# An emission order written out as a table, the mixing shifts on compute engines, and W3 loaded ahead, in a gated long-convolution and MLP-mixer kernel

## The chip, the cores and the metric

The kernel runs on one core of one Trainium2 chip. The metric is the device time in microseconds (us) of one execution. A core has five engines, each with an in-order instruction queue of its own: TensorE (PE in the profile, with its weight loads as PEld), VectorE (DVE), ScalarE (ACT), GpSimd (POOL) and SyncE (SP). In this kernel SP issues every transfer. Engines wait for one another through semaphores.

## The reference, cut to what matters

With S = 2048 positions, D = 640 channels and F = 1536 hidden channels, in bf16:

```python
x = A_q
g = sigmoid((x * gate_w).sum(-1, keepdims=True))
# A: a 4-tap shift convolution of k, times v, then a causal long convolution over S
k_shift = sum(k_pad[:, t:t + S, :] * shift_k[:, 3 - t] for t in range(4))
kv = k_shift * v
y = irfft(rfft(kv, 2S) * rfft(ssm_k, 2S))[:S] + kv * ssm_D
a = x * y
# B: a token mixer and an MLP, each with a residual
h = gelu(layernorm(x) @ w1)             # four groups of 160 channels
hs = concat(h shifted by 1, -1, 2, -2 positions, group by group) @ w2
x1 = x + hs
b = x1 + gelu(layernorm(x1) @ w3) @ w4
out = g * a + (1 - g) * b
```

## The kernel before, in words

Positions are laid out as 128 partitions by 16 slabs, so a slab is 128 rows of 640 channels. The work falls into two arms that share x and meet at the output. Every operation is a node with a short name, and the names are those of the table in the change.

**The mixer arm.** `q0` to `q7` load x into QX. `st0.s` takes the statistics of slab s, on DVE or on ACT; `rs0.s` forms the inverse deviation of two slabs on POOL; `xn0.s` normalizes on DVE into a ring of three XN buffers. `tr0.c.i` transposes two slabs on PE and `te0.c.i` copies the result out of PSUM, for four chunks c of four slabs each. `W1.c.n` is a 128x512 tile of x @ w1, five matmuls each, and `g1.c.n` is its gelu on ACT. The last 32 channels of each 160-channel group are gathered in MIX, and `mx c.gi` brings them into GST at their shifted position (lines 828 to 833: twenty small SBUF-to-SBUF transfers issued by SP). `W2.s` multiplies a slab by w2 (ten matmuls) and `add s` adds it to x on DVE. `gt.c`, `z c` and `gate0` to `gate2` make the gate.

**The MLP.** `st1`, `rs1` and `xn1` normalize again; `xt1.c.i` transposes a slab by a DMA transpose (line 757) into one of two XNT buffers; `W3.c.f` (line 967) are 48 tiles of five matmuls 128x512; `g2.c.f` their gelus; `W4.s.j` (line 980) 32 tiles of twelve matmuls 128x320; `w4e s.j` (line 986) adds them into QX on DVE. `xo s` scales x1 by 1 - g beforehand. `w3` and `w4` load the weights into the tile W34.

**The convolution.** A two-level Fourier transform as matmuls. Its tables are generated on the chip: `ang`, `and`, `abs` and `sin` fill F1, `m3*` fill M3; the scratch for the angles lies in W34. `trh` (line 914) transposes the filter, `trhe` copies it out, `h1.s.h` (line 936) is its first level, `he` copies it out and `hw c` writes it to DRAM. `km` (lines 1024 and 1029), `ka` (line 1033) and `kv` (line 1036) form kv on DVE, eight operations of 1280 columns for each pair of slabs; `x1`, `xe` and `xw` are the first level of kv. `rh` and `rx` (line 1080) read both spectra back in another layout; `h2` and `x2` (line 1053) are the second level; `sw` (line 1096) swaps partition neighbours by a transfer; `pq` (line 1113) multiplies the spectra on DVE; `pv` (line 1053) is the first inverse level; `ve` copies it out; `vw` writes it to DRAM and `rv` reads it back. `iv s` (line 1149) is the last inverse level of slab s, four matmuls; `y s` (line 1154) multiplies it by the gate and by x, which `rq` (line 1141) has loaded again; `ya s` (line 1159) adds it into QX; `st s` stores the slab.

**What sets the order.** `Plan.schedule` is a list scheduler that runs when the program is built. It gives each node a rank from due times (`PAR`) and from 928 corrections (`ADJ`), keeps for each engine the nodes that are ready, and at each step starts the ready node of lowest rank on a free engine; it also chooses ACT or DVE or POOL where a node has alternatives, and the buffer of each ring. All transfers share one model of a DMA path at a node's rate, with 350 ns to issue and 1900 ns of latency. The nodes are then emitted in the order of their modelled starts, so each engine's queue has that order. PSUM is a ring of eight banks; a tile `w=2` takes two neighbours.

Of the kernel before, what the change touches and what calls it, by code (L numbers as in the profile page):

```python
# [20 lines left out]
class Ring:  # L21
    def __init__(self, name, n):
        self.name, self.n = name, n
        self.free = list(range(n))


    def take(self, w):
        if w == 1:
            one = [i for i in self.free if self.n != 8 or i ^ 1 not in self.free] or self.free
            i = min(one)  # L30
            self.free.remove(i)
            return i
        i = min(i for i in self.free if i % 2 == 0 and i + 1 in self.free)
        self.free.remove(i)
        self.free.remove(i + 1)
        return i

    def can(self, w, keep):
        if len(self.free) < w + keep:
            return False  # L40
        return w == 1 or any(i % 2 == 0 and i + 1 in self.free for i in self.free)


class Buf:
    __slots__ = ("ring", "idx", "users", "gate", "w")

    def __init__(self, ring, gate=(), w=1):
        self.ring, self.idx, self.users, self.gate, self.w = ring, None, 0, tuple(gate), w


class Node:
    __slots__ = ("name", "alts", "fn", "deps", "succ", "bufs", "mode", "tgt", "after", "bytes", "rate",
                 "npend", "ready", "start", "end", "eng", "rank", "seq", "lat", "sts")


DMA_ISSUE = 350.0
DMA_LAT = 1900.0


def lat_of(n):  # L60
    return 230.0 if "PE" in n.alts else (60.0 if n.bytes else 170.0)


class Plan:
# [3 lines left out]
    def add(self, name, alts, fn, deps=(), bufs=(), mode=None, tgt=None, after=0.0, nbytes=0, rate=370.0):  # L68
# [8 lines left out]
        n.bufs, n.mode, n.tgt, n.after, n.bytes, n.rate = list(bufs), mode, tgt, after, nbytes, rate  # L77
        n.seq = len(self.nodes)
        self.nodes.append(n)
        return n  # L80

    def dma(self, name, fn, nbytes, deps=(), bufs=(), q="SP", rate=370.0, tgt=None, after=0.0):
        return self.add(name, {q: DMA_ISSUE}, fn, deps, bufs, None, tgt, after, nbytes, rate)

    def schedule(self, par):
        nodes = self.nodes
        rings, bufs = {}, {}
        for n in nodes:
            n.succ, n.eng, n.start, n.end = [], None, None, None
            for b in n.bufs:  # L90
                bufs[id(b)] = b
                rings[id(b.ring)] = b.ring
                b.users, b.idx = 0, None
        for r in rings.values():
            r.free = list(range(r.n))
        for n in nodes:
            for b in n.bufs:
                b.users += 1
            n.npend = len(n.deps)
            n.ready = n.after  # L100
            n.lat = lat_of(n)
            for d in n.deps:
                d.succ.append(n)
        topo, cntp = [n for n in nodes if not n.deps], {id(n): len(n.deps) for n in nodes}
        for n in topo:
            for s in n.succ:
                cntp[id(s)] -= 1
                if cntp[id(s)] == 0:
                    topo.append(s)
        assert len(topo) == len(nodes)  # L110
        for n in reversed(topo):
            dur = min(n.alts.values())
            if n.bytes:
                dur += DMA_LAT + n.bytes / n.rate
            n.rank = min((s.rank for s in n.succ), default=400000.0) - n.lat - dur
            if n.tgt is not None:
                g = par[n.tgt[0]]
                n.rank = min(n.rank, 1000.0 * (g[0] + sum(x * y for x, y in zip(g[1:], n.tgt[1:]))))
        for n in nodes:
            if "PE" in n.alts:  # L120
                for d in n.succ:
                    if "PE" not in d.alts and any(b.ring.name == "ps" and b in n.bufs for b in d.bufs):
                        d.rank = min(d.rank, n.rank + 1000.0 * par["evac"][0])
        for i, (a, _) in ADJ.items():
            nodes[i].rank += 1000.0 * a
        keep = int(par["keep"][0] + 0.5)
        vpen, mpen = 1000.0 * par["vpen"][0], 1000.0 * par["mpen"][0]
        engs = ("PE", "ACT", "DVE", "POOL", "SP")
        free = {e: 0.0 for e in engs}
        mode = {"PE": None, "ACT": None}  # L130
        pend = {e: [] for e in engs}
        ev = []
        cnt = 0
        dma_free = 0.0
        left = len(nodes)
        rel = []

        def push(n):
            for e in n.alts:
                k = n.rank + (vpen + 1000.0 * ADJ.get(n.seq, (0, 0))[1] if e == "DVE" and len(n.alts) > 1 else 0.0)  # L140
                bisect.insort(pend[e], (k, n.seq, n))
            heapq.heappush(ev, n.ready)

        for n in nodes:
            if n.npend == 0:
                push(n)
        t = 0.0
        while left:
            while rel and rel[0][0] <= t:
                b = heapq.heappop(rel)[2]  # L150
                b.ring.free.extend(range(b.idx, b.idx + b.w))
            prog = True
            while prog:
                prog = False
                for e in engs:
                    if free[e] > t:
                        continue
                    best, bk = None, None
                    for k, _, n in pend[e]:
                        if bk is not None and k >= bk:  # L160
                            break
                        if n.ready > t:
                            continue
                        ok = True
                        short = e == "PE" and n.alts["PE"] < 700.0
                        seen = {}
                        for b in n.bufs:
                            if b.idx is None:
                                k2 = id(b.ring)
                                if not b.ring.can(b.w, seen.get(k2, 0) + (keep if short and b.ring.name == "ps" else 0)):  # L170
                                    ok = False
                                    break
                                seen[k2] = seen.get(k2, 0) + 1
                        if not ok:
                            continue
                        if e == "PE" and n.mode != mode["PE"]:
                            k += mpen
                        if e == "ACT" and n.mode is not None and n.mode != mode["ACT"]:
                            k += 3000.0
                        if bk is None or k < bk:  # L180
                            best, bk = n, k
                    if best is None:
                        continue
                    n = best
                    prog = True
                    for e2 in n.alts:
                        pend[e2] = [x for x in pend[e2] if x[2] is not n]
                    dur = n.alts[e]
                    if e == "PE":
                        if n.mode != mode["PE"]:  # L190
                            dur += 95.0
                        mode["PE"] = n.mode
                    if e == "ACT" and n.mode is not None:
                        if n.mode != mode["ACT"]:
                            dur += 1300.0
                        mode["ACT"] = n.mode
                    n.eng, n.start = e, t
                    for b in n.bufs:
                        if b.idx is None:
                            b.idx = b.ring.take(b.w)  # L200
                    free[e] = t + dur
                    if n.bytes:
                        s0 = max(t + dur, dma_free)
                        dma_free = s0 + n.bytes / n.rate
                        n.end = dma_free + DMA_LAT
                    else:
                        n.end = t + dur
# [195 lines left out]
def kernel(  # L403
# [16 lines left out]
    nc = tc.nc  # L420
# [150 lines left out]
    def f_w2(e):  # L571
        pass
# [624 lines left out]
```

## Time and profile before

| | us |
|---|---|
| three runs | 243.5, 244.31, 247.2 (median 244.31) |
| the profiled execution, device time | 244.2 |
| its span, first to last instruction | 242.4 |

| engine | busy us | share of the span |
|---|---|---|
| PE | 217.4 | 90% |
| DVE | 190.7 | 79% |
| ACT | 163.9 | 68% |
| POOL | 45.8 | 19% |

The page lists 65.11 MB moved by the transfers, 269 GB/s on average. The device time of the profiled execution is 1.8 us above its span. In the rows below, a line of the wait view names the engine and line that waited, what it waited for, and the sum, the count and the longest in us; a line of the timeline gives start, length, engine, line, operation and the number of merged instructions; a line of the window view gives a stretch of time and how long each engine was busy in it. Ends of matmuls are modelled, so neighbouring rows of PE overlap a little.

### The profile page before, as it was taken

What the parts mean: (1) busy time and instruction counts of PE and PEld (TensorE: products, weight loads), DVE (VectorE), ACT (ScalarE), POOL (GpSimd) and SP (SyncE); (2) the same over time, 40 slices, a digit from 0 to 9 for tenths busy, and PEclk for the clock granted to TensorE, in tenths of its full rate; (3) what the DMA queues carried; (4) which work ended last, traced back from release to release, by engine and by line L of the source; (5) the groups of instructions that cost most, each with busy time, mean ns of one, the idle gap of its engine ahead of it and who ended that gap; (6) DMA issues with size and microseconds to landing.
All of it is one profiled execution on the core that took longest, in us unless ns stands there. A gap on an engine that the chain in (4) does not pass through costs nothing.

```text
span 242.4 us, 4444 instructions
## 1 busy us (share of the span) xinstructions
PE 217.4 (90%) x1645; PEld 125.3 (52%) x1645; DVE 190.7 (79%) x337; ACT 163.9 (68%) x247; POOL 45.8 (19%) x116
## 2 busy tenths in 40 slices
PE   0499999999759999999899998899999899998993
PEld 0495565556433565765464354453334456465671
DVE  8879999997981799999994524999658795086995
ACT  5989999999774578779858943767999661420000
POOL 6694542164040037600000000000000000000000
PEclk9999999999997999999999999999999999999998
DMA  5999986039499989978399869999899464799973
GB/s 164 385 400 282 260 290 218 3 88 286 84 361 376 268 224 293 300 251 313 121 303 371 321 178 332 353 284 377 287 390 341 171 219 173 248 397 343 303 244 139
DMA packets 50070, 65.11 MB, mean 269 GB/s; under 512 B 19584, under 2 KB 36737, under 8 KB 49664
## 3 DMA queue, kind: packets, MB, share of 16 engines
q1 hardware_dynamic: 50048, 64.82, 82.7%
q8 instruction: 13, 0.21, 0.4%
q14 instruction: 9, 0.07, 0.1%
HBM read 37.03 MB, written 18.35 MB: 228 GB/s over the span
## 4 chain that ended last, share of the span: by engine, by line
PE 51%; DVE 19%; DMA 18%; ACT 5%; issue 3%; POOL 1%; DVEq 0%; SPq 0%; ACTq 0%; POOLq 0%
PE PS L967 17%; PE PS L980 12%; PE PS L1053 6%; DMA CJ<-in_A_q_dram 4%; DMA RK<-GXD 4%; PE PS L794 4%; PE PS L936 4%; DVE RK L1154 4%; DMA R<-R 4%; DMA W<-in_B_w_dram 3%; PE PS L881 3%; PE PS L914 3%; DMA XNT<-XN 3%; DVE RK L1029 2%; DVE RK L1033 2%
## 5 line engine op out<-in xcount | busy, mean ns | idle before, releaser
L967 PE MATMUL PS<-XNT,W 128*128 128x512 bf16 x240 | 58.3, 388 | 3.4 <-DMA W<-in_B_w_dram 2.7
L980 PE MATMUL PS<-W,RG 128*128 128x320 bf16 x384 | 56.3, 299 | 0.2 <-DVE RK L1154 0.2
L542 ACT CAST SX<-PS 128x640 bf16<-128x640 f32 (+1 forms) x65 | 47.2, 769 | 10.1 <-DMA R<-R 4.2
L980 PEld LDWEIGHTS <-RG 128*128 128x128 bf16 x384 | 36.7, 98 | 18.8 <-issue 4.7
L971 ACT ACTIVATE RG<-PS 128x512 bf16<-128x512 f32 x48 | 28.9, 602 | 24.6 <-PE PS L967 24.4
L967 PEld LDWEIGHTS <-W 128*128 128x128 bf16 x240 | 22.8, 100 | 32.6 <-issue 8.1
L1113 DVE TENSOR_TENSOR SX<-SX,R 128x2048 bf16<-128x2048 bf16 x20 | 24.0, 1219 | 3.4 <-DMA R<-R 2.8
L936 PE MATMUL PS<-KV,F 128*128 128x320 bf16 x128 | 24.2, 299 | 1.6 <-DVE SX L546 0.7
L794 PE MATMUL PS<-XNT,R 128*128 128x512 bf16 x100 | 24.1, 379 | 0.7 <-ACT R L801 0.6
L881 PE MATMUL PS<-R 128*128 128x320 bf16 x160 | 23.4, 299 | 1.5 <-DVE QX L888 1.5
L546 DVE CAST SX<-PS 128x640 bf16<-128x640 f32 (+1 forms) x19 | 18.0, 947 | 6.6 <-PE PS L936 2.8
L986 DVE SCALAR_TENSOR_TENSOR QX<-PS,ZG,QX 128x320 bf16<-128x320 f32 x32 | 17.2, 546 | 6.4 <-PE PS L980 6.4
L542 ACT CAST KV<-PS 128x1024 bf16<-128x1024 f32 x16 | 15.9, 1014 | 8.6 <-PE PS L1053 8.5
L1154 DVE SCALAR_TENSOR_TENSOR RK<-PS,ZG,CJ 128x640 bf16<-128x640 f32 x16 | 13.4, 877 | 9.4 <-ACT RG L971 6.5
L881 PEld LDWEIGHTS <-R 128*128 128x128 bf16 x160 | 15.7, 98 | 8.7 <-issue 1.7
L1033 DVE TENSOR_TENSOR RK<-RK 128x1280 bf16<-128x1280 bf16 x24 | 19.7, 822 | 0.5
L1029 DVE TENSOR_TENSOR RK<-RK,CJ 128x1280 bf16<-128x1280 bf16 x24 | 19.2, 818 | 0.0
L936 PEld LDWEIGHTS <-F 128*128 128x128 bf16 x128 | 12.3, 97 | 10.7 <-issue 3.4
L750 DVE TENSOR_SCALAR XN<-QX,MV,RS 128x640 bf16<-128x640 bf16 x32 | 13.5, 444 | 3.9 <-POOL RS L743 2.6
L1053 PEld LDWEIGHTS <-M 64*64 64x64 bf16 x320 | 7.5, 105 | 15.6 <-issue 7.2
L765 PE MATMUL PS<-IDN,XN 128*128 128x128 bf16 x80 | 6.3, 231 | 9.7 <-DVE XN L750 9.7
L1053 PE MATMUL PS<-RK,M 64*64 64x512 bf16 x160 | 13.0, 384 | 1.9 <-DMA RK<-GXD 1.8
(97 smaller groups left out, 276.2 us busy)
## 6 DMA issues: line engine op xcount, KB each, us to landing
GHD<-SX SPq DMA_DIRECT2D x8, 640.0 KB, 6.7
GXD<-SX SPq DMA_DIRECT2D x8, 640.0 KB, 4.3
RK<-GHD SPq DMA_DIRECT2D x4, 1280.0 KB, 8.2
RK<-GXD SPq DMA_DIRECT2D x4, 1280.0 KB, 8.7
R<-R SPq DMA_DIRECT2D x8, 640.0 KB, 8.7
VD<-KV SPq DMA_DIRECT2D x4, 1280.0 KB, 6.2
RK<-VD SPq DMA_DIRECT2D x8, 640.0 KB, 6.3
W<-in_B_w_dram SPq DMA_DIRECT2D x2, 1920.0 KB, 12.8
```

The costliest lines, as they stand in the source:

```text
L542: nc.scalar.copy(out=o, in_=i)
L794: nc.tensor.matmul(ps(pb), lhsT=lhsT, rhs=XNT[:, xb.idx, k, :], start=(k == 0), stop=(k == DT - 1))
L881: nc.tensor.matmul(ps(pb)[:, j, 0:DH], lhsT=gst_ap(k, s), rhs=W2[:, k, j * DH:(j + 1) * DH], start=(k == 0), stop=(k == DT - 1))
L936: nc.tensor.matmul(ps(pb)[:, j, 0:DH], lhsT=F1[:, h, s, :], rhs=src[:, s, ds], start=True, stop=not dterm)
L967: nc.tensor.matmul(ps(pb), lhsT=W3[:, k, f0 * P:(f0 + 1) * P], rhs=XNT[:, xb.idx, k, :], start=(k == 0), stop=(k == DT - 1))
L971: gns.append(pl.add("g2.%d.%d" % (c, f0), {A: act_p(512)}, lambda e, f0=f0, pb=pb, gb=gb: nc.scalar.activation(out=GTP[:, gb.idx, f0 % 4, ...
L980: nc.tensor.matmul(ps(pb)[:, 0:DH], lhsT=GTP[:, gbs[f // 4].idx, f % 4, i * P:(i + 1) * P], rhs=W4[:, f, j * DH:(j + 1) * DH], start=(f == ...
L1029: m = pl.add("km%d.%d.%d" % (c, u, j), {V: dve(2 * D, .52)}, lambda e, src=src, cj=cj, tb=tb: nc.vector.tensor_tensor(out=TMP[:, tb.idx].r ...
L1033: prev = pl.add("ka%d.%d.%d" % (c, u, j), {V: dve(2 * D, .52)}, lambda e, tb=tb: nc.vector.tensor_tensor(out=acc, in0=acc, in1=TMP[:, tb.i ...
L1053: nc.tensor.matmul(pt[64 * C:64 * C + 64, R, :], lhsT=M3[64 * R:64 * R + 64, m, :], rhs=rhs_fn(R, C), start=start, stop=stop)
L1113: nc.vector.tensor_tensor(out=PQ[:, qb.idx], in0=XS[:, sb.idx].unsqueeze(1).to_broadcast([P, 2, 1024]), in1=HH[:, hhb.idx, u], op=ALU.mult)
L1154: nc.vector.scalar_tensor_tensor(out=GY[:, yb.idx].rearrange("p (j d) -> p j d", j=2), in0=ps(pb)[:, :, 0:DH], scalar=G32[:, s:s + 1], in1 ...
```

## The change

1. `Plan.schedule` with `PAR` and `ADJ` is gone. `Plan.order` reads a table of 925 words in the order of emission: name, engine, buffer numbers. Engines, buffers and order of every operation come from it.
2. The sixteen mixing shifts (with their four wrap-arounds) are copies on POOL (12) or DVE (4) in the place of twenty transfers.
3. The scratch for the angles and for M3 is moved so that `w3` overwrites nothing that the tables still need, and `w3` no longer waits for the tables. It stands in the table behind `v1` and ahead of the first `xt1`. The loads of the first 128 rows of each group of w2 become one transfer of four.
4. The sine of an angle is taken before its absolute value, which is then formed in place.
5. Fields for the issue time and the number of descriptors are added to transfers; they do not reach the program.

```diff
-    def schedule(self, par):
...
-        return sorted(nodes, key=lambda n: (n.start, n.seq))
+    def order(self, table):
+        by = {n.name: n for n in self.nodes}
+        out = []
+        for w in table.split():
+            name, e, *slots = w.split("/")
+            n = by[name]
+            n.eng = ENG[e]
+            for b, k in zip(n.bufs, slots):
+                b.idx = int(k)
+            out.append(n)
+        assert len(out) == len(self.nodes)
+        return out
...
+ORDER = """
+bpi/V iw/G is/G cw/V cs/V ang0/V and0/V sin0.1/A ang2/V ang3/V ang1/V q1/S st0.3/A and1/V sin1.1/A and3/V st0.2/V sin3.1/A
+abs1/A sin1.0/A abs0/A q0/S st0.1/V st0.0/V idn/G misc/G m3i0/G rs0.2/G xn0.2/V/0 m3i2/G rs0.0/G xn0.3/V/1 kz/G/0 h4/S trh4/P/0
+trhe4/V/0 h0/S trh0/P/2 m3i3/G m3i1/G sin0.0/A tr0.0.2/P/4/0/0/1 te0.0.2/A/4/0 h3/S trh3/P/6 xn0.0/V/2 xn0.1/V/0
+tr0.0.0/P/0/0/2/0 te0.0.0/A/0/0 trhe0/V/2 and2/V sin2.1/A m3b/V trhe3/V/6 h1/S trh1/P/2 w1/S W1.0.2/P/0/0 W1.0.0/P/1/0 m3i4/G
...
+h1.15.0/P/0/0 he.15.0/A/0/0 w3/S gate1/A W1.2.1/P/4/0 h1.9.0/P/6/2 he.9.0/A/6/2 g1.2.1/A/4 xn1.2/V/1 xn1.3/V/0 xt1.0.1/S/0/0
...
+he.14.1/A/6/0 W3.0.5/P/1/0/0 g2.0.5/A/1/0 ka0.1.0/V/1/0 kv2/V/0 mx2.2/G st1.8/A g1.3.0/A/0 W3.0.7/P/4/0/0 W3.0.6/P/1/0/0
...
+x2.3.2/P/2/1/0 x2e.3.2/A/2/0 pq.3.3/V/2/1/1 pv.3.3/P/6/1/1 ve.3.3/A/6/1 w4e11.0/V/0 pq.3.0/V/1/0/1 vw2/S/0 W3.3.6/P/0/1/0
+g2.3.6/A/0/0 ve.3.1/A/4/1 pv.3.0/P/2/0/1 pq.3.2/V/0/1/1 pv.3.2/P/6/1/1 ve.3.2/A/6/1 W3.3.4/P/0/1/0 g2.3.4/A/0/0 ve.3.0/V/2/1
+vw3/S/1 W3.3.7/P/2/1/0 g2.3.7/A/2/0 W3.3.3/P/0/1/1 W3.3.2/P/2/1/1 W3.3.0/P/3/1/1 g2.3.0/A/3/1 g2.3.3/A/0/1 W3.3.5/P/4/1/0
+g2.3.5/A/4/0 g2.3.2/A/2/1 w4e10.1/V/1 W3.3.1/P/1/1/1 g2.3.1/A/1/1 W4.14.0/P/0/1/0/3 w4e14.0/V/0 W4.0.0/P/1/1/0/3 w4e0.0/V/1
+rv0/S/0 iv0/P/6/0 y0/V/6/0/1 iv1/P/4/0 y1/V/4/1/1 ya1/V/1 ya0/V/0 W4.14.1/P/0/1/0/3 w4e14.1/V/0 rv1/S/1 iv3/P/2/1 y3/V/2/2/0
...
+w4e0.1/V/0 rv5/S/3 iv12/P/6/1 iv10/P/4/3 rq5/S/1 st2/S iv13/P/2/1 y10/V/4/0/1 ya10/V/0 st6/S st9/S iv11/P/0/3 y11/V/0/1/1
+ya11/V/1 rq6/S/0 y12/V/6/2/0 st8/S st7/S st3/S st4/S st1/S st14/S st10/S st15/S st11/S st0/S st5/S ya12/V/2 st12/S y13/V/2/3/0
+ya13/V/3 st13/S
+"""
...
-    NANG = GEN[:, 0:4096].bitcast(I32)
-    NABS = GEN[:, 4096:8192].bitcast(F32)
+    I1f = I1.rearrange("p h t d -> p (h t d)")
+    NANG = I1f.bitcast(I32)
+    NABS = I1f.bitcast(F32)
...
-    an3, ani, sn3 = (I1f[:, i * 6 * MB:(i + 1) * 6 * MB].bitcast(dt) for i, dt in enumerate((F32, I32, F32)))
+    an3, ani, sn3 = gt_(3 * MB, F32), gt_(3 * MB, I32), gt_(3 * MB, F32)
...
-                nc.sync.dma_start(out=GST[a:b, 4, lo:hi, 1:129], in_=MIX[a:b, lo - sh:hi - sh, :])
+                g.tensor_copy(out=GST[a:b, 4, lo:hi, 1:129], in_=MIX[a:b, lo - sh:hi - sh, :])
...
     ldw3 = pl.dma("w3", lambda e: nc.sync.dma_start(out=W3, in_=B_w3.rearrange("(k p) f -> p k f", p=P)), D * Fh * 2,
-                  f1n + [m3n], after=24000.0, rate=400.0)
+                  [], rate=400.0, ndesc=640)
...
-    plan = pl.schedule(PAR)
     with tc.manual_schedule():
-        for n in plan:
+        for n in pl.order(ORDER):
             n.fn(n.eng)
```

More of the change, by code (lines that the diff above doesn't have):

```diff
@@ L23, in __init__ @@
         self.name, self.n = name, n
[L24 to L41, printed above, removed]
 class Buf:
-    __slots__ = ("ring", "idx", "users", "gate", "w")
+    __slots__ = ("ring", "idx", "gate", "w")
     def __init__(self, ring, gate=(), w=1):
-        self.ring, self.idx, self.users, self.gate, self.w = ring, None, 0, tuple(gate), w
+        self.ring, self.idx, self.gate, self.w = ring, None, tuple(gate), w
 class Node:
[L52 to L61, printed above, removed]
+    __slots__ = ("name", "alts", "fn", "deps", "bufs", "mode", "bytes", "rate", "iss", "ndesc", "eng", "seq", "sts")
 class Plan:
@@ L238, in act_p @@
+ENG = {"P": "PE", "A": "ACT", "V": "DVE", "G": "POOL", "S": "SP"}
 def act_p(n):
@@ L1042 @@
     i1n = [pl.dma("tri%d" % h, lambda e, h=h: nc.sync.dma_start_transpose(
-        out=I1[:, h], in_=F1[:, h].rearrange("p t c -> p (t c)")), P * P * T1 * 2, f1n + [m3n], [], rate=XT_RATE, after=60000.0) for h in range(2)]
+        out=I1[:, h], in_=F1[:, h].rearrange("p t c -> p (t c)")), P * P * T1 * 2, f1n + [m3n], [], rate=XT_RATE, iss=2060.0, ndesc=1600) for h in range(2)]
     xpe, xwr = step1("x", KV, GXD, lambda s: [kvn[s]], False)
```

335 lines of the change are left out of this document (128 added, 207 removed), and 145 rows, old and new, of tables (ADJ, PAR).

## The prediction

> **What bounds the kernel now.** I read the page's engine shares first, then its chain of work that ended last, then a table of stages that I cut at events of PE's timeline.
>
> ```profile
> span 242.4 us, 4444 instructions
> ...
> PE 217.4 (90%) x1645; PEld 125.3 (52%) x1645; DVE 190.7 (79%) x337; ACT 163.9 (68%) x247; POOL 45.8 (19%) x116
> ...
> PE 51%; DVE 19%; DMA 18%; ACT 5%; issue 3%; POOL 1%; DVEq 0%; SPq 0%; ACTq 0%; POOLq 0%
> ```
>
> PE is busy for 217.4 of 242.4 us, and half of the chain is PE: the change leaves PE's work as it is, so it can gain only from the 25.0 us in which PE does nothing, and from PE work that runs slower than it could. Where those are, the stages show (columns after the stretch: its length, PE, PEld, DVE, ACT, POOL busy, granted clock, DMA share, GB/s):
>
> ```profile
> 0.00:9.67 9.67, 0.00 (x0) 0.00 (x1) 8.59 (x33) 6.61 (x12) 5.55 (x30) 1.00 0.73 240
> 9.67:18.34 8.67, 8.67 (x101) 8.59 (x102) 6.35 (x16) 7.49 (x8) 7.82 (x26) 1.00 1.03 404
> 18.34:72.79 54.45, 49.14 (x396) 29.67 (x394) 50.60 (x115) 50.84 (x84) 21.47 (x41) 1.00 0.69 208
> 72.79:81.13 8.34, 8.34 (x32) 3.51 (x33) 1.51 (x3) 3.70 (x7) 0.28 (x1) 0.80 1.15 373
> 81.13:200.78 119.65, 115.13 (x884) 60.68 (x883) 97.19 (x129) 89.81 (x130) 10.63 (x20) 1.00 0.89 282
> 200.78:212.16 11.38, 11.38 (x71) 6.48 (x68) 2.88 (x4) 3.68 (x6) 0.00 (x0) 1.00 0.65 225
> 212.16:238.20 26.04, 24.72 (x171) 16.35 (x169) 22.12 (x37) 1.79 (x3) 0.00 (x0) 1.00 0.88 307
> 238.20:242.40 4.20, 0.02 (x1) 0.00 (x0) 1.48 (x4) 0.00 (x0) 0.00 (x0) 0.78 0.44 155
> ```
>
> PE idles 9.67 us at the start, 5.31 us (54.45 less 49.14) up to the first W3 tile at 72.79, 4.52 us from there to the last `pv` at 200.78, 1.32 us in the tail, and 4.2 us behind its last matmul. The named waits of PE:
>
> ```profile
> PE PS L765 <- DVE XN L750: 9.7, 1, 9.7
> PE PS L967 <- DMA W<-in_B_w_dram: 2.7, 1, 2.7
> PE PS L1053 <- DMA RK<-GXD: 1.8, 2, 1.1
> PE PS L881 <- DVE QX L888: 1.5, 1, 1.5
> ```
>
> Apart from the start and the late W3 load they are crumbs. The span is thus: start, then PE nearly full to the last `pv`, then a tail of 41.6 us (242.4 less 200.8).
>
> **The start.** Before, PE waits for the first normalized slabs:
>
> ```profile
> 1.07 0.86 DVE L1002 MEMSET RK<- 1x960 int32 x1 [0.16 <-issue]
> ...
> 2.76 0.97 DVE L615 TENSOR_SCALAR W<-W 128x128 int32<-128x128 f32 x4
> ...
> 16.17 2.17 PE L914 MATMUL PS<-IDN,RG 128*128 128x128 bf16 x32
> 18.18 3.40 PE L794 MATMUL PS<-XNT,R 128*128 128x512 bf16 x15
> ```
>
> The table has `trh4` first on PE, which needs only the third transfer, `h4`. The transfers bring 240 GB/s in the first stretch, 404 in the second; `q1`, `q0` and `h4` are 1.18 MB, so PE can begin near 6.7. It then stops for `xn0.2`: DVE does four `ang` (0.97 each), three `and`, three `st0` and two `xn` first, and I put them in a row to about 10.7. The memset of 0.86 goes to POOL, in nobody's way. By the same adding up the four chunk-0 slabs are in XNT at 14.8 and the first W1 tile starts near 15.0, against 18.18, but with one of the five `trh` (2.17 us for 32 matmuls, so about 1.0) still to do: **-2.2 us**.
>
> **W3 ahead.** Here the load, not its input, was last:
>
> ```profile
> 54.10 4.40 SPq L757 DMA_TRANSPOSE XNT<-XN  x2
> ...
> 65.15 0.54 SPq L893 DMA_DIRECT2D W<-in_B_w_dram  x1
> ```
>
> ```profile
> 72.79 8.34 PE L967 MATMUL PS<-XNT,W 128*128 128x512 bf16 x30 [2.74 <-DMA W<-in_B_w_dram]
> ...
> 205.68 6.64 PE L967 MATMUL PS<-XNT,W 128*128 128x512 bf16 x30
> ```
>
> ```profile
> 60.64 0.45 DVE L750 TENSOR_SCALAR XN<-QX,MV,RS 128x640 bf16<-128x640 bf16 x1 [1.34 <-DMA XNT<-XN]
> ```
>
> Issued at 65.15, it lands 7.6 us later. In the table it stands ahead of the first `xt1`, without the wait for the tables, so by 54.10 it would be issued, and lands some ten us before its tiles. **-2.7 us** for the wait. The thirty matmuls behind that idle time took 8.34 us at a granted clock of 0.80; the same thirty take 6.64 at 205.68: **-1.7 us**. What is late next is chunk 0's last transpose: `xn1.5` reuses the buffer of `xn1.3` and waits for its transfer, as the last row shows for before (1.34 us on DVE). I leave 1 us for it below.
>
> **The mixing shifts.** Twenty transfers leave SP and the queue. Copies of this shape are not in the trace. Nearest on POOL, and, for collisions, POOL's small power and DVE's multiply (shortest, median and longest in ns):
>
> ```profile
> L704 POOL COPY R<-R x5: 286/292/1044, 9.4 to 11.1; 128x128 bf16<-128x128 bf16 x5
> L992 POOL COPY CJ<-RK x4: 752/818/874, 23.5 to 25.7; 128x640 bf16<-128x640 bf16 x4
> L743 POOL TENSOR_TENSOR RS<-VE,NHALF x16: 703/728/1272, 7.9 to 102.3; 128x2 f32<-128x2 f32 x16
> L1029 DVE TENSOR_TENSOR RK<-RK,CJ x24: 810/819/820, 34.8 to 120.8; 128x1280 bf16<-128x1280 bf16 x24
> ```
>
> On SP, one of the transfers that go, and on DVE the normalizing of 640 elements:
>
> ```profile
> 24.30 0.77 SPq L828 DMA_DIRECT2D R<-R  x1
> ```
>
> ```profile
> L750 DVE TENSOR_SCALAR XN<-QX,MV,RS 128x640 bf16<-128x640 bf16 x32 | 13.5, 444 | 3.9 <-POOL RS L743 2.6
> ```
>
> A shift moves 512 elements of 32 partitions: between 0.29 us (128 elements) and 0.82 (640); I take 0.65, nearer to the second. Twelve are 8 us on an engine that is busy for 45.8, so nothing on the path, unless the `rs1` behind them come late; at worst 0.82 each, 10 us. The four on DVE take at most 0.44 each, 1.8 us. SP is freed of twenty issues of 0.6 to 0.8 us, 13 us; that costs and gains nothing by itself, since PE names no shift as its releaser, but it is what lets `w3` and the `xt1` out earlier. The bounds for the whole edit are -1.5 us (PE's wait for `add`, last row of its waits) and +1.
>
> The same 2-element operation takes 0.70 us or up to 1.27 on POOL, while DVE's 1280-column multiply stays between 810 and 820 ns. The Trainium skill ("SBUF — State Buffer", section "Who interferes with whom") has GpSimd's only port pair shared with VectorE as an exclusive lock, so that the one that comes second blocks wholly. By that rule the trace agrees that POOL is the one stretched; no row here shows a DVE operation stretched. Were it DVE that waited behind twelve copies, DVE would lose up to 8 us, which is counted in the slower rival.
>
> **The order itself.** Two things can be counted from the table. First, behind the last `pv` it leaves 7 W3, 8 W4 and 16 `iv`; before:
>
> ```profile
> 200.78 5.06 PE L980 MATMUL PS<-W,RG 128*128 128x320 bf16 x36
> ...
> 212.16 1.25 PE L1149 MATMUL PS<-RK,I 128*128 128x320 bf16 x8
> ```
>
> 36 + 24 + 72 matmuls of W4 were left (eleven tiles) and eight W3 tiles. So three W4 (5.06) and one W3 (6.64/6 = 1.1) move ahead of the last `pv`: **+6.1 us** until it. The tail doesn't shrink by as much, because it is DVE's:
>
> ```profile
> 212.70:239.00 26.30, 22.92 (x39) 1.00 0.88 306
> ```
>
> ```profile
> 220.43 1.68 DVE L1154 SCALAR_TENSOR_TENSOR RK<-PS,ZG,CJ 128x640 bf16<-128x640 f32 x2 [2.48 <-DMA CJ<-in_A_q_dram]
> ...
> 230.20 1.68 DVE L1154 SCALAR_TENSOR_TENSOR RK<-PS,ZG,CJ 128x640 bf16<-128x640 f32 x2 [0.43 <-DMA CJ<-in_A_q_dram]
> ```
>
> From the first `y` DVE is busy 22.92 of 26.30 us, and 11.4 us pass before it (`ve`, `vw3`, `rv0`), which the change leaves alone. After: one `w4e` fewer (0.5) and no wait of 2.9 for `rq`, except that `rq6` is issued only behind `y15`, for which I give back 1.2: **-2.2 us**.
>
> Second, the small waits. Before had 7.1 us of them ahead of the last `pv` (5.31 + 4.52 less the 2.74 of W3). Walking the table with the rows above I find room for 1.0 at `xn1.5`, 0.5 at `x1.13` (behind `kv12`), 0.8 at `pv.0.2` (the swap follows `rx0`, with 4 us of PE work between), 1.0 at `h2.3`/`x2.2`, 0.3 in crumbs: 3.6, so **-3.5**. This is the softest term: its bounds are -7.1 (none left) and, by the largest like sum in the trace, +7.1 (twice as many).
>
> **Sum.** 242.4 - 2.2 - 2.7 - 1.7 + 6.1 - 2.2 - 3.5 = 236.2 of span; the profiled execution lies 1.8 above its span (244.2 against 242.4): **238.0 us**, 2.5% under that execution; the median, 244.31, stands at the same place. Some 2% (4.9 us) is what a measurement of this kernel tells from no change.
>
> **The rivals.**
>
> *The crumbs come back.* A new order trades one set of small waits for another; with the 7.1 us of before the sum is 239.7 + 1.8 = 241.5, no change. For it: DVE and ACT are over 90% busy in 18 to 73, so every engine's queue leans on the others there. Against it: before, SP's queue held back transfers that were ready, and the table's clears it.
>
> *Slower: DVE's kv chain.* All four `rh` and `rx` write where k was, so they wait for the last `km`; `kv14` ends the chain.
>
> ```profile
> DVE KV L1036 <- DMA KV<-in_A_v_dram: 6.4, 1, 6.4
> ```
>
> ```profile
> 80.00:128.00 48.00, 46.73 (x76) 1.00 0.89 258
> ```
>
> Before, DVE waited 6.4 us for `v1`, then was full. At 0.75 us for each of the 64 operations and the rows of the others, the table's DVE work up to `kv14` comes to some 112 us (an estimate), and `h2` needs it at about 124 (its place on PE, some 134, less 10 for two transfers). So 12 us of waits are free; beyond that each costs PE a microsecond, since its queue stands at the first `h2`. In the table `add` and `w4e` stand among the `km`, in one queue: if DVE waits there 12 + 17 us, through late `W2` and blocked ports, the time is 238 + 17 less the crumbs, about 251. Against: `v1` goes out ahead of `w3`.
>
> *The first levels gain nothing* (PE's early start only shifts its pause): 238.0 + 2.2 = 240.2, inside the second case.
>
> **How the numbers follow.** Forecast, with fewer crumbs: 0.57, times 232 to 239.4. The crumbs come back: 0.29, 239.4 to 246. Slower: 0.14, above 246, mostly above 249. The low end is the sum with none left, 232.7 + 1.8 = 234.5, less 2.5 for a tail without a wait of DVE. The range leaves out the slowest and little else: 232 to 246.
>
> **What the profile would show.** Right: PE's first instruction near 6.7 and the first W1 near 15; no PE wait for W, the first W3 near 66 at full clock; no R to R transfer of 16 or 32 KB; last `pv` at 196 to 198; a tail near 39.5 with DVE full. Wrong: a DVE wait of over 5 us between `kv2` and `kv14`; PE waiting for `rh` or `rx` for over 2 us; POOL copies well over 0.82 us with `xn1` behind them; or a first `iv` more than 12 us behind the last `pv`.

## The result, and the profile after

The changed kernel takes **233.74 us** (median of 4 runs, 232.8 to 234.85) against 244.35 for the kernel before: a ratio of 0.9579, with a 95% interval of 0.952 to 0.9638. It is faster by 4.2%, 10.6 us. Medians are of all runs, and a ratio leaves out single runs that lie more than 1.5% above the fastest of their kernel. The profiled execution took 234.0 us, its span is 231.7. The forecast was 238.0 with a range of 232 to 246, so the sign and the range hold, and the size was short by 4 us.

The page's head, engine shares and the chain that ended last, after:

```profile
span 231.7 us, 4405 instructions
...
PE 212.7 (92%) x1626; PEld 124.7 (54%) x1645; DVE 198.1 (85%) x346; ACT 152.5 (66%) x238; POOL 56.0 (24%) x133
...
PE 25%; DVE 11%; DMA 7%; ACT 4%; issue 2%; SPq 0%; DVEq 0%; ACTq 0%
```

PE has the same 1645 weight loads, and 19 of its matmul records are missing, so its 212.7 us are the same work as the 217.4 of before. Of the 4.7 us between them 1.7 are the part at half clock, and about 0.9 are the missing records; the rest is taken up under the crumbs below. Idle time of PE was 25.0 us before and is 19.0 now, so idle rows show 6.0 of the 10.7 us of span.

The stages after, cut at the same events (length, PE, PEld, DVE, ACT, POOL busy, granted clock, DMA share, GB/s):

```profile
6.98:14.94 7.96, 7.81 (x84) 7.61 (x85) 7.86 (x22) 6.40 (x9) 5.88 (x18) 1.00 1.03 398
14.94:65.18 50.24, 49.34 (x402) 30.52 (x409) 46.33 (x105) 45.26 (x78) 30.14 (x65) 1.00 0.85 266
65.18:193.00 127.82, 125.79 (x947) 67.67 (x957) 113.19 (x156) 91.36 (x139) 17.20 (x32) 1.00 0.89 276
193.00:204.56 11.56, 10.95 (x63) 5.71 (x61) 1.54 (x3) 5.25 (x9) 0.00 (x0) 1.00 0.66 228
204.56:223.90 19.34, 18.85 (x138) 13.19 (x135) 18.90 (x32) 0.00 (x0) 0.00 (x0) 1.00 0.96 321
223.90:231.70 7.80, 0.00 (x0) 0.00 (x0) 4.35 (x8) 0.00 (x0) 0.00 (x0) 0.74 0.82 299
```

PE starts at 6.98; the first W1 product is at 14.94, the first W3 at 65.18, the last `pv` ends at 193.00. From 14.94 to 193.00 PE idles for 0.90 + 2.03 us, where it idled for 9.8. The clock is full in all of it: the stretch behind the first W3 product, at 0.80 before, is gone. PE's waits, and the first W3 tiles in PE's timeline:

```profile
PE PS L691 <- DMA RG<-in_A_ssm_k_dram: 7.0, 1, 7.0
PE PS L830 <- DVE SX L890: 0.6, 3, 0.2
PE PS L757 <- ACT RG L748: 0.6, 1, 0.6
```

```profile
14.94 2.32 PE L569 MATMUL PS<-XNT,R 128*128 128x512 bf16 x9
...
65.18 10.96 PE L744 MATMUL PS<-XNT,W 128*128 128x512 bf16 x49
```

No wait for W, none for QX above 0.5, none for GXD. 49 matmuls in 10.96 us are 0.22 each, full clock; before, 30 took 8.34.

### The profile page after: what moved, and what is told of

It reads as the page before. It is cut to its first block, busy times and chain, and to the rows that moved or that the text cites. A ratio compares the mean times of both kernels' runs of the same rounds, so it can differ in the third digit from the quotient of the medians.

```text
span 231.7 us, 4405 instructions
## 1 busy us (share of the span) xinstructions
PE 212.7 (92%) x1626; PEld 124.7 (54%) x1645; DVE 198.1 (85%) x346; ACT 152.5 (66%) x238; POOL 56.0 (24%) x133
## 5 line engine op out<-in xcount | busy, mean ns | idle before, releaser
L318 ACT CAST SX<-PS 128x640 bf16<-128x640 f32 (+1 forms) x67 | 49.7, 770 | 22.0 <-PE PS L713 8.7
L744 PE MATMUL PS<-XNT,W 128*128 128x512 bf16 x228 | 55.2, 379 | 0.7 <-issue 0.2
L748 ACT ACTIVATE RG<-PS 128x512 bf16<-128x512 f32 x48 | 27.5, 601 | 11.0 <-PE PS L744 10.2
L810 DVE TENSOR_TENSOR RK<-RK 128x1280 bf16<-128x1280 bf16 x24 | 20.3, 844 | 0.5
L806 DVE TENSOR_TENSOR RK<-RK,CJ 128x1280 bf16<-128x1280 bf16 x24 | 19.4, 820 | 0.0
L322 DVE CAST SX<-PS 128x640 bf16<-128x640 f32 (+1 forms) x17 | 15.7, 936 | 4.0 <-PE PS L713 3.5
L658 PEld LDWEIGHTS <-R 128*128 128x128 bf16 x160 | 15.5, 98 | 6.6 <-issue 0.3
L498 ACT ACTIVATE RG<-QX 128x640 bf16<-128x640 bf16 x16 | 11.8, 736 | 5.3 <-DVE QX L665 5.1
L318 ACT CAST KV<-PS 128x1024 bf16<-128x1024 f32 x14 | 14.1, 1022 | 1.4 <-PE PS L830 1.3
L569 PEld LDWEIGHTS <-R 128*128 128x128 bf16 x100 | 9.6, 98 | 9.7 <-issue 0.7
L665 DVE SCALAR_TENSOR_TENSOR QX<-PS,QX 128x640 bf16<-128x640 f32 x16 | 12.9, 818 | 1.6 <-PE PS L658 0.8
L320 ACT ACTIVATE R<-PS 128x1024 bf16<-128x1024 f32 x12 | 12.0, 1024 | 3.5 <-PE PS L830 3.5
```

The costliest lines, as they stand in the source:

```text
L318: nc.scalar.copy(out=o, in_=i)
L322: nc.vector.tensor_copy(out=o, in_=i)
L569: nc.tensor.matmul(ps(pb), lhsT=lhsT, rhs=XNT[:, xb.idx, k, :], start=(k == 0), stop=(k == DT - 1))
L658: nc.tensor.matmul(ps(pb)[:, j, 0:DH], lhsT=gst_ap(k, s), rhs=W2[:, k, j * DH:(j + 1) * DH], start=(k == 0), stop=(k == DT - 1))
L744: nc.tensor.matmul(ps(pb), lhsT=W3[:, k, f0 * P:(f0 + 1) * P], rhs=XNT[:, xb.idx, k, :], start=(k == 0), stop=(k == DT - 1))
L748: gns.append(pl.add("g2.%d.%d" % (c, f0), {A: act_p(512)}, lambda e, f0=f0, pb=pb, gb=gb: nc.scalar.activation(out=GTP[:, gb.idx, f0 % 4, ...
```

## The experiments

A theory and two rivals stood at the beginning. **Mine**: the gain is the sum of the prediction's terms (earlier start, W3's wait and slow clock, fewer small waits, a shorter tail) and the shifts on engines are no more than a condition. **Rival one**: the shifts are a main part of it, since they free SP. **Rival two**: W3 ahead gains little by itself, another input being as late. All times beside a run of the kernel before on the same chip.

### The shifts, alone in each order

Back on SP in the kernel after (every `mx` word gets `/S`):

```diff
-                g.tensor_copy(out=GST[a:b, 4, lo:hi, 1:129], in_=MIX[a:b, lo - sh:hi - sh, :])
+                nc.sync.dma_start(out=GST[a:b, 4, lo:hi, 1:129], in_=MIX[a:b, lo - sh:hi - sh, :])
```

> The kernel after, with the 16 mixing shifts back as transfers on SP's queue (two DMAs where one wraps), issued at the table's places; everything else is the table's. Theory 1 (the shifts on engines only clear SP's queue; the gain comes from the earlier start, from W3 and from fewer small waits): within 2 us of after, 234 to 236, since the next xt1 and v transfers stand well ahead of their use and PE names no shift as its releaser. Rival (the shifts on engines are a main part of the gain, because their issues of 0.6 to 0.8 us, 13 us in all, held back what stood behind them): at least 4 us slower than after, 238 or more, with PE waiting for XNT or W. If the POOL copies themselves cost something (DVE operations beside them stretch from 820 to as much as 1122 ns), up to 1 us faster than after.

Measured: 253.99 us, 1.0378 of before (1.033 to 1.0425): 20 us slower than after and 9 slower than before. My theory missed this by far, and the rival, too, was short. SP's waits, and the issue of W3 on SP (at 46.53 after):

```profile
SPq L604 <- ACT R L577: 11.1, 2, 7.8
```

```profile
61.81 0.59 SPq L670 DMA_DIRECT2D W<-in_B_w_dram  x1
```

and PE's waits with two stretches of the same run:

```profile
PE PS L658 <- DMA GHD<-SX: 8.5, 1, 8.5
...
PE PS L658 <- DMA R<-R: 5.7, 2, 4.5
```

```profile
38.20:46.70 8.50, 0.02 (x1) 0.01 (x1) 0.23 (x2) 2.81 (x4) 4.60 (x8) 0.73 0.78 316
46.70:60.00 13.30, 13.17 (x121) 9.39 (x124) 9.95 (x19) 6.37 (x10) 1.48 (x2) 0.79 0.19 70
```

SP stands for 11.1 us at two shifts whose gelu (L577) isn't done; what stands behind them, loads of w2's rows, `hw`, further shifts and W3, goes out late. PE stops for 8.5 us in its first W2 tile, ahead of the two matmuls of ten that read the shifted rows, and its clock is 0.79 for the 13 us behind that. The row names `hw` (GHD from SX), which W2 does not read. The shift that this tile reads, `mx1.3`, was issued at 37.23, behind `v0`, `k1` and `hw1`, and landed at 46.63, 0.17 us after that `hw` and just before PE goes on (last column: us from issue to landing):

```profile
RK<-in_A_k_dram SPq DMA_DIRECT2D x1, 1120.0 KB, 10.6
GHD<-SX SPq DMA_DIRECT2D x1, 640.0 KB, 10.3
R<-R SPq DMA_DIRECT2D x1, 32.0 KB, 9.4
```

Two causes were possible: SP's order, or the time that a shift takes as a transfer. So the same transfers were issued from POOL's queue:

```diff
-                nc.sync.dma_start(out=GST[a:b, 4, lo:hi, 1:129], ...)
+                nc.gpsimd.dma_start(out=GST[a:b, 4, lo:hi, 1:129], ...)
```

> The kernel after, with the 16 mixing shifts as transfers again, at the table's places, but issued from POOL's own queue in place of SP's. With them on SP's queue the same kernel took 254.0, 20 more than after, PE waiting 8.5 us for a swap (GHD) that stood behind a shift and 5.7 for shifts themselves. Theory 1 (in-order queue: a shift that waits for its gelu keeps back the swaps, W3 and the transposes behind it on SP): with SP free of them most of the 20 us goes, 235 to 240, W3 is issued at about 46 again and no PE wait names GHD. Rival (latency: a shift as a transfer lands 2 us and more behind its issue, where the copy takes 0.7, and the table leaves no room for that): PE's waits for R from R stay, 6 us or more over after, 240 or more.

Measured: 234.28 us, 0.9583 (0.9505 to 0.966): the kernel after, within 0.6 us. W3's issue is at 46.67 again. `mx1.3` is issued at 31.58 and lands 3.3 us later, so it gains 5.7 us by its place in a queue and 6.1 by a shorter way; which of the two counts for more was not separated. Of PE's waits 1.0 us is left for a shift:

```profile
R<-R POOLq DMA_DIRECT2D x1, 32.0 KB, 3.3
```

```profile
PE PS L658 <- DMA R<-R: 1.0, 1, 1.0
```

So whether a shift is a copy or a transfer makes no difference that can be told; in this order it may not stand on SP's queue. Then the other way round, the shifts on engines (the 12 and 4 of the table) in the order of before, written out as a table:

```diff
-                nc.sync.dma_start(out=GST[a:b, 4, lo:hi, 1:129], in_=MIX[a:b, lo - sh:hi - sh, :])
+                g.tensor_copy(out=GST[a:b, 4, lo:hi, 1:129], in_=MIX[a:b, lo - sh:hi - sh, :])
```

> The kernel before, its order kept, with the 16 mixing shifts alone made copies on POOL (12) and DVE (4) in place of transfers. Theory 1 (the shifts on engines are worth nothing by themselves: PE names none as its releaser; the 18 to 20 us that the shifts on SP cost in the table's order come from an order made for engines, in which SP's queue stands still behind a shift that waits for its gelu): within 1.5 us of before. Rival (the shifts on SP cost before, too, by holding up the swaps and transposes behind them): 3 us faster or more.

Measured: 244.93 us, 1.0028 (0.9996 to 1.0061), no change. SP had stood at a shift in the old order, too, for as long as in the new one, as its waits in the kernel before show:

```profile
SPq L828 <- ACT R L801: 10.8, 1, 10.8
```

Taking that wait away gained nothing, so what stood behind it there was not what PE lacked. What a shift costs on SP's queue goes by what stands behind it.

### W3 ahead, alone in each order

In the kernel after, W3's word moved behind the four transposes:

```diff
-w3/S gate1/A ... xt1.0.1/S/0/0 ... xt1.0.0/S/0/1 ... xt1.0.2/S/0/2 ... xt1.0.3/S/0/0
+gate1/A ... xt1.0.1/S/0/0 ... xt1.0.0/S/0/1 ... xt1.0.2/S/0/2 ... xt1.0.3/S/0/0 w3/S
```

> The kernel after, with the transfer of W3 issued behind the four transposing transfers xt1 of the first pair in place of ahead of them (SP's order alone). After, W3 is issued at 46.5 and the first W3 product runs at 65.2; the last xt1 is issued at 60.3. Theory 1 (the earlier W3 is worth a wait of 2.7 and a slow clock of 1.7): W3 is issued at about 61 and lands in some 7 us or more, so PE waits 3 to 4 us at the first W3 product and runs on at half clock after it: 4 to 5.5 us slower than after, 238 to 239.5. Rival (W3 is not what bounds the start of the second part, other inputs of that stage are as late, or small waits soak it up): within 1 us of after.

Measured: 241.96 us, 0.9886 (0.9832 to 0.994), 8.2 more than after. The theory's mechanism, at twice its size:

```profile
71.43 4.88 PE L745 MATMUL PS<-XNT,W 128*128 128x512 bf16 x11 [6.19 <-DMA W<-in_B_w_dram]
76.53 8.57 PE L745 MATMUL PS<-XNT,W 128*128 128x512 bf16 x38 [0.22 <-issue]
```

W3, issued at 61.45, lets the product begin at 71.43, ten us later and not seven; the wait is 6.2, and 11 matmuls at 0.44 in place of 0.22 add 2.4. In the order of before, with the scratch moved out of W3's way (not to the same places as in after) and the word `w3/S` moved behind `v0/S`:

```diff
-                  f1n + [m3n], after=24000.0, rate=400.0)
+                  [], after=24000.0, rate=400.0)
```

> The kernel before, its order kept, with W3's transfer alone issued ahead: it waits for no W1 product any more (its scratch and the two arrays that lay in its place are moved, as in the kernel after) and stands behind the first transfer of v on SP's queue. Theory 1 (the wait of 2.7 us for W and the half clock behind it, 1.7, are worth 4.4 because nothing else of that stage is later): 4.4 us faster than before, 240.4 by 244.8. Rival (the transposed x of the first pair is nearly as late: its last transfer is issued at 62.5 and such a one takes some 8 us, against the first W3 product at 72.8): a gain of 1 to 2 us, PE then waiting for XNT, the clock still falling. If W3's 1.97 MB in the middle of the first stage delay the other inputs: no gain or a loss.

Measured: 241.06 us, 0.9866 (0.982 to 0.9911): 3.3 us faster, between the two. The first W3 product and PE's largest wait behind the start:

```profile
70.19 6.64 PE L774 MATMUL PS<-XNT,W 128*128 128x512 bf16 x30
```

```profile
PE PS L860 <- DMA RK<-GXD: 2.6, 3, 1.3
PE PS L688 <- DVE QX L695: 2.2, 1, 2.2
```

The wait for W is gone and 30 matmuls take 6.64 in place of 8.34, the 1.7 in full. Of the wait's 2.7 only 1.6 came through (from the first W1 to the first W3 product: 53.0 us, before 54.6). Of the 1.1 lost, PE's wait for `add`, grown from 1.5 to 2.2, accounts for 0.7. No wait of PE names XNT: rival two's transposes were not what was late. By the events in the table below this execution is 4.3 us ahead at the first `h2` (1.0 of it already at the first W1, which the edit doesn't explain) and 2.6 at the end.

### Both parts in the old order

The two edits just shown for the old order, in one kernel:

```diff
+                  [], after=24000.0, rate=400.0)
+                g.tensor_copy(out=GST[a:b, 4, lo:hi, 1:129], in_=MIX[a:b, lo - sh:hi - sh, :])
```

> The kernel before, its order kept, with both: W3's transfer ahead and the mixing shifts on POOL and DVE. What is then left between this kernel and after is the order of the operations (and the earlier start, which is part of it). Theory 1: the sum of the two runs beside it, 3 to 5 us faster than before (240 to 242), so that the order gives the other 6 to 8 us. Rival (the two need the other, or together they are the change and the order hardly matters): 8 us faster than before or more.

Measured: 243.41 us, 0.995 (0.9908 to 0.9993): 0.9 faster, less than either theory. PE's events in the six kernels, from their timelines:

| | first W1 | first W3 | first `h2` | first `iv` | span |
|---|---|---|---|---|---|
| before | 18.18 | 72.79 | 130.95 | 212.16 | 242.4 |
| W3 ahead | 17.16 | 70.19 | 126.65 | 208.75 | 239.8 |
| shifts on engines | 17.52 | 73.43 | 131.96 | 213.01 | 243.6 |
| both | 17.85 | 73.44 | 129.91 | 211.11 | 241.0 |
| after | 14.94 | 65.18 | 128.27 | 204.56 | 231.7 |
| after, other tail (below) | 14.69 | 65.16 | 128.26 | 203.88 | 229.1 |

With the shifts on POOL and DVE in the old order the first stage (W1 to W3) is 55.6 to 55.9 us long, 54.6 before, and W3 is ready and waits for PE. After, the same stage takes 50.2. Between "both" and after lie 9.3 us of span, and the order is nearly all that differs (which operation stands where, and on which of its engines; besides it, w2's rows come in one transfer and not four, the sine stands ahead of the absolute value, and some scratch lies elsewhere). **The order is the main part of the gain**; the two parts named beside it bring 1 us without it. Of the 9.3 us after is 2.9 ahead at the first W1, 5.4 more at the first W3, and 1.0 more behind it.

### The start

`trh4`, `trhe4` and `trh0` moved behind `tr0.0.2`:

```diff
-h4/S trh4/P/0 trhe4/V/0 h0/S trh0/P/2 m3i3/G m3i1/G sin0.0/A tr0.0.2/P/4/0/0/1 ...
+h4/S h0/S m3i3/G m3i1/G sin0.0/A tr0.0.2/P/4/0/0/1 trh4/P/0 trhe4/V/0 trh0/P/2 ...
```

> The kernel after, with the first two groups of 16 filter transposes (trh4, trh0) moved behind the first transposes of x in PE's queue, so that PE begins when x's first statistics are done, at about 9.7, as before. Theory 1 (the early start is worth its 2.2 us because PE is then busy to the end): 2 us slower than after, 235.5 to 236.5, and the first W1 product at about 17 in place of 14.9. Rival (PE's early start only moves its pause, since the first W1 waits for x, not for the filters; my second case): within 0.5 us of after, the first W1 still at 14.9.

Measured: 236.02 us, 0.9651 (0.9614 to 0.9687), 2.3 more than after, as expected. The first W1 product:

```profile
17.70 2.32 PE L570 MATMUL PS<-XNT,R 128*128 128x512 bf16 x9 [0.30 <-ACT XNT L319]
```

It is 2.8 later, and the end 1.9 later in the span: the start is worth its term, since PE is full behind it.

### The slack of DVE's kv chain

`v1` moved behind `xt1.1.1` on SP:

```diff
-hw6/S/0 v1/S cj1/G ... xt1.1.0/S/1/1 ... xt1.1.1/S/1/2
+hw6/S/0 cj1/G ... xt1.1.0/S/1/1 ... xt1.1.1/S/1/2 v1/S
```

> The kernel after, with the transfer of v1, which stands at 46 on SP's queue, issued some 25 us later, behind a transposing transfer of the second pair, so that DVE, whose chain of km and kv is one queue, waits for it at kv4 as it did before (6.4 us then). This tests how much slack that chain has ahead of the first h2 on PE. By my working (12 us of slack): 0 to 1 us slower than after, 233.5 to 235. By what the trace of after shows (the last kv at 118.0, two transfers, the first h2 at 128.3, no more than some 2 us between them): the wait less 2 us, so about 4 us slower, with PE waiting for RK or running short of W3 and W4 work at about 128.

Measured: 234.98 us, 0.9626 (0.9575 to 0.9678). Both numbers were wrong, since v1 landed sooner than reckoned and DVE waited 1.1 us and not 6:

```profile
81.40 0.83 DVE L814 TENSOR_TENSOR KV<-RK,KV 128x1280 bf16<-128x1280 bf16 x1 [1.06 <-DMA KV<-in_A_v_dram]
```

```profile
129.33 0.84 PE L831 MATMUL PS<-RK,M 64*64 64x512 bf16 x12
```

The first `h2` starts at 129.33, at 128.27 after: 1.06 us of DVE's time are 1.06 of PE's, and 1.2 of the median (the intervals overlap; the profiled executions differ by 2.5, of which 1.4 is a wait of PE at 177.88, behind a late swap). So there are no 12 us of slack. DVE's lateness reaches PE long before `rh`, by an `add` that stands in DVE's queue behind `kv4`:

```profile
85.94 0.43 PE L714 MATMUL PS<-KV,F 128*128 128x320 bf16 x2 [1.24 <-DVE QX L666]
```

After, this wait is 0.34. That a later kv costs PE its whole lateness was seen for 1.1 us, and only once.

### The tail: DVE, the transfers, or both

First DVE: 14 of the 16 `ya` (the add of the gated convolution into QX; not a D*v term, as the expectation calls it) on POOL, and `rq6` ahead of `st2`:

```diff
-ya1/V/1 ya0/V/0 ... rq5/S/1 st2/S ... ya11/V/1 rq6/S/0
+ya1/G/1 ya0/G/0 ... rq5/S/1 rq6/S/0 st2/S ... ya11/V/1
```

> The kernel after, with 14 of the 16 products ya (the D*v term of the outputs, bf16, 1 column group each) on POOL in place of DVE, and the last transfer of q (rq6) issued ahead of an output store in place of behind it. In the tail, after, DVE is busy 23.18 of the last 23.50 us, so it sets the end. Theory 1 (the tail is bound by DVE): each ya taken off DVE in the last stretch saves its own duration; the part of them that lies in the tail gives 2 to 3 us, 231 to 232. Rival (the tail is bound by the chain from iv over gate to store, or POOL, at some 1 us each, becomes late): same as after, or slower by 1 to 2 us.

Measured: 233.61 us, 0.9549 (0.9502 to 0.9597): nothing that can be told (0.7 us by the ratios, inside the intervals). But the adds only went from one full engine to another:

```profile
207.39 17.66 POOL L937 TENSOR_TENSOR QX<-QX,RK 128x640 bf16<-128x640 bf16 x13 [82.56 <-issue]
```

POOL takes about 1.4 us for each and is full to 225.05, and PE ends at 223.47 as after (223.87); DVE has pauses and waits for PE. So the reading that the tail is DVE's was not enough. Of the tail's other loads, the DMA share of 0.96 stands out. So the transfers, alone: `rq2` to `rq7` into the first half of R, free by then, issued behind `vw1`:

```diff
-in1=QR[:, qb.idx, s % 2, :]          # two places in CJ
+in1=qr()[:, s % 2, :]                # rq0, rq1 there, rq2 to rq7 in R1[:, 0:7680]
```

> The kernel after, with the last six transfers of q (320 KB each) moved out of the tail: they go into the first half of R, free behind the second levels, and stand on SP's queue behind the second transfer of v to DRAM, at about 187, where the DMAs are busy for 0.24 to 0.53. In the tail (203 to 230) they are busy for 0.95 and more. Theory 1 (three things are full at once in the tail: DVE, the DMAs and, to 223, PE, so that taking one away alone does nothing, as with ya on POOL): within 1 us of after. Rival A (the DMAs alone set the end; ya on POOL did nothing because of them): 2 to 3 us faster. Rival B (transfers ahead of the last vw hold it up, and the first iv): 1 to 2 us slower.

Measured: 233.61 us, 0.9539 (0.9473 to 0.9605): nothing again (1.0 us by the ratios, inside the intervals). Then both, with the stores spread and a W4 tile last on PE (the end of the table):

```diff
-W4.0.1/P/0/1/0/3 w4e0.1/V/0 ... iv12/P/6/1 iv10/P/4/3 ... iv13/P/2/1 ... iv11/P/0/3 ... st8/S st7/S st3/S st4/S
+... st3/S st2/S st1/S rv5/S/3 ... iv12/P/6/1 ... iv13/P/4/1 ... iv10/P/2/3 ... iv11/P/6/3 ... W4.0.1/P/0/1/0/3 ya10/V/2 w4e0.1/V/0
```

> The kernel after with both: the six transfers of q ahead of the tail and 12 of the 16 ya on POOL; besides, in the tail's order, the stores stand among the work as soon as their rows are ready, and the last product on PE is one of W4 (evacuation 0.55 us) in place of four iv in a row (0.88 and 0.49 each). Theory 1 (DVE, DMAs and PE bound the tail together): only now does the end move, by 2 to 3 us from after: 231 to 232, DVE's last operation at about 225.5 in place of 228.4. Rival (something else, as the 640 KB transfers of v or the last store's own 3 us, sets the end): within 1 us of after.

Measured: 235.14 us, 0.9611 (0.9559 to 0.9662). The new order had a fault. DVE's and PE's timelines:

```profile
222.97 0.55 DVE L765 SCALAR_TENSOR_TENSOR QX<-PS,ZG,QX 128x320 bf16<-128x320 f32 x1 [3.71 <-POOL QX L940]
```

```profile
224.36 0.70 PE L930 MATMUL PS<-RK,I 128*128 128x320 bf16 x4 [3.47 <-DVE RK L935]
224.90 3.23 PE L759 MATMUL PS<-W,RG 128*128 128x320 bf16 x12
```

An evacuation stood behind a `ya` that had gone to POOL and writes the same rows; DVE waited for POOL, PE for DVE. Mended:

```diff
-iv14/P/4/2 y14/V/4/2 iv15/P/2/2 y15/V/2/3 ya14/G/2 ya15/G/3 ... W4.15.1/P/1/1/0/3 w4e15.1/V/1
+iv14/P/4/2 y14/V/4/2 iv15/P/2/2 y15/V/2/3 ... W4.15.1/P/1/1/0/3 w4e15.1/V/1 ya14/G/2 ya15/G/3
```

> The run before this one (q's transfers ahead, 12 of 16 ya on POOL, another order of the tail) had one fault of its own: the evacuation w4e15.1 on DVE stood behind ya15, which had gone to POOL and writes the same rows, so DVE waited 3.7 us for POOL and PE 3.5 us for DVE. Here w4e15.1 stands ahead of ya15, and nothing else is changed. Theory 1 (DVE, DMAs and PE bound the tail together): without that wait the end moves by what was expected, DVE's and POOL's last operations at about 225.5 in place of 228.4: 230.5 to 232, 2 to 3 us under after and 13 under before. Rival (the last transfers or another wait set the end): within 1 us of after, 233 to 234.5.

Measured: **232.76 us**, 0.9494 (0.9424 to 0.9563), with the profiled execution at 231.12 and its span at 229.1. It is the fastest of all, some 2 us under after by the two ratios, though their intervals overlap. The same stretch of 23.5 us in the four kernels, in the order after, `ya` on POOL, q ahead, all of it:

```profile
204.90:228.40 23.50, 18.51 (x135) 12.93 (x133) 23.18 (x39) 0.00 (x0) 0.00 (x0) 0.98 0.97 331
```

```profile
204.90:228.40 23.50, 18.57 (x137) 13.14 (x135) 18.94 (x25) 0.00 (x0) 19.05 (x14) 0.99 0.93 330
```

```profile
204.90:228.40 23.50, 19.55 (x143) 13.69 (x140) 22.26 (x38) 0.00 (x0) 0.00 (x0) 0.96 0.80 269
```

```profile
204.90:228.40 23.50, 17.93 (x130) 12.44 (x128) 20.07 (x26) 0.00 (x0) 16.60 (x12) 0.97 0.77 262
```

In the first, DVE (23.18) and the transfers (0.97) are full together; the second relieves DVE and fills POOL, the third relieves the transfers and keeps DVE; the last has less of both, DVE's last operation ends at 225.95 and not at 228.4, and the span is 2.6 us shorter. Not all of that is the tail. The first `iv` starts at 204.56, 204.83, 205.60 and 203.88, although the third and the fourth kernel are the same up to there, so executions differ by over 1 us ahead of the tail; from the first `iv` to the end it is 27.2, 27.1, 26.5 and 25.2 us. The last tail is thus 2.0 us shorter. That both loads had to go for it is argued: this kernel also has another order of the tail's end, and how much that alone gives was not tried.

## Why the prediction was right, and where it was off

The span fell by 10.7 us (242.4 to 231.7). Term by term:

| step | predicted | measured | how known |
|---|---|---|---|
| start | -2.2 | -2.2 (14.94 for 18.18, one `trh` of 1.0 left) | shown: +2.3 when undone |
| wait for W3 | -2.7 | -2.7, no such wait in the trace | shown, together with the next row: +8.2 when undone in the new order, -3.3 alone in the old |
| half clock behind it | -1.7 | -1.7 (full clock) | shown: 8.34 to 6.64 in the old order |
| W3 and W4 moved ahead | +6.1 | +6.0 (36 W4 at 0.136, 5 W3 at 0.22) | counted |
| tail | -2.2 | -2.9 (41.6 to 38.7) | reason half right |
| crumbs | -3.5 | -7.2, the rest of the sum | mis-sized |

- **Right**: the bound (PE between 15 and 193), the start, W3 ahead and its clock, and the count of moved products. The shifts on engines cost and gain nothing by themselves, as put; but "it is what lets `w3` and the `xt1` out earlier" was worth more than I saw. A shift took 0.71 us on POOL (0.50 to 1.30) and 0.26 on DVE, for 0.65 and at most 0.44 reckoned; the long ones, a sign of being wrong, held up nothing that PE waited for. The prediction bounded the shifts by -1.5 and +1; in the new order their place off SP is worth 20. The edit and the order can't be priced apart.
- **Mis-sized: the crumbs.** Bounds -7.1 to +7.1, taken -3.5 by walking the table, measured -7.2. I had sized them on PE's idle rows, 7.1 us before, 2.9 after, which is 4.2; so "none left" was no bound. Of the 2.9 some 0.9 are gaps of 0.05 us where a record is missing, so idle rows give rather 5.1, and some 2 don't stand in them: a matmul's end is modelled, a 128x320 row is 0.30 long where the next starts 0.136 later, so a wait of up to 0.16 hides in it. The starts show it: from one matmul to the next of another or the same line W2's take 154.6 ns on average before and 136.4 after, W4's 151.9 and 142.9 (worked out from all starts between the first W1 and the last `pv`; the idle rows are a part of these distances). The Trainium skill ("Perfetto Trace Analysis", section "Tensor Engine Instruction (MATMUL, LD_WEIGHTS)") says that the end of a TensorE instruction is an estimate from its size; this trace agrees, 0.30 against 0.136. That the sum of such gaps falls is measured; that they were small waits for evacuations is argued, and no run took them away singly. The term as a whole is a remainder of the sum, not a measurement of its own.
- **Wrong: the slack of 12 us** in the kv chain, which carried the slower rival's price. It put the last `kv` at 112 and the first `h2` at 134; they came at 118.0 and 128.3. Of the six us at the first, 4.5 are the 64 operations taken at 0.75 us, where the rows of before show 0.82. Between the two the second `rh`, issued at 118.1, lands at 127.0, which leaves 1.3 us. The rival didn't come because the table gives DVE the v1 in time (its 6.4 us wait is gone), not because there was room.
- **Half right: the tail.** "It is DVE's" missed that the transfers are full at the same time and that PE is nearly full to 223.9 (18.51 us of it), and moving work from DVE to POOL gained nothing. The 1.2 us given back for `rq6` were not needed: DVE is busy 23.18 of 23.50 and never waits for it, which more than covers the 0.7 by which the term was short.
- **The rival "crumbs come back"**, at 0.29, would have shown as PE idle of 7 us between 15 and 193; 2.9 were left.

## What to carry to other kernels

An order for in-order queues and the choice of queue for each operation are one decision: the same edit is worth nothing, 1 us or 20 by what stands behind it in its queue, so try an edit in the old order and undo it in the new one before giving it a price. Where a stage has two full resources, taking load off one may show nothing, and so may load that only moves to a third; look at every share in that stretch, DMA included, before naming its bound. Size small waits by the distance between starts, not by idle rows, when the ends are modelled.

## What the hardware showed that I had not expected

**DVE and POOL in each other's way.** The prediction said that no row showed a DVE operation stretched. The add of two bf16 tiles (128x640) on DVE with POOL idle (after), and beside POOL's adds (the last kernel), min/median/max in ns:

```profile
L936 DVE TENSOR_TENSOR QX<-QX,RK x16: 483/491/493, 207.0 to 227.9; 128x640 bf16<-128x640 bf16 x16
```

```profile
L940 POOL TENSOR_TENSOR QX<-QX,RK x12: 1392/1394/1644, 205.6 to 224.0; 128x640 bf16<-128x640 bf16 x12
...
L940 DVE TENSOR_TENSOR QX<-QX,RK x4: 864/1116/1214, 206.3 to 224.7; 128x640 bf16<-128x640 bf16 x4
```

A factor of 2.3, while DVE's `y`, with one operand in PSUM, stays at 0.87 to 0.88 in both. The Trainium skill ("SBUF — State Buffer", "Who interferes with whom") has a DVE instruction with two SBUF inputs contend with GpSimd's reads, and one with a single SBUF input, outside its two-port modes, not; `ya` and `y` agree here. In the changed kernel itself it is small, and either side can be the one stretched: L810's adds reach 1122 ns beside POOL's shifts, where none took over 825 before, while a multiply of L806, also with two inputs in SBUF, kept 799 ns within a shift that took 1297 on POOL, where six of the other eight of its size take 606 to 730.

**The clock falls after short pauses.** Each of these was seen once. A pause of PE of 2.15 us (W3 ahead in the old order) left the clock full: the ten matmuls behind it took 1.52 us. One of 2.74 (before) halved it for some 3.3 us, one of 3.47 (the tail's first order) had twelve matmuls take 3.23 in place of 1.79, and one of 8.5 (the shifts on SP) left it at 0.79 on average for 13 us. The Trainium skill ("TensorE: Matmul & The Clock Gate", "Part 1: The HAM clock gate (the 'warmup' mystery)") puts the fall behind an idle window of about 3.4 us that runs freely; a pause of 2.74 was enough here.
